# Scores of the first two batches from float32 q and k, instead of from rounded parts and rests

## The chip, the cores and the metric

The kernel runs on one core of a Trainium2 chip. The metric is the device time of one execution in microseconds (us), the median of several executions. A core has five engines that run side by side, each with its own queue taken in order: TensorE (PE in the profile, its weight loads PEld), VectorE (DVE), ScalarE (ACT), GpSimd (POOL) and SyncE (SP), which here issues all transfers (DMA).

## The reference, cut to what matters

Three layers follow each other: causal attention with a decay (4 batches, 8 heads, 576 positions, 64 numbers per head), a gated feed-forward layer of 2304 tokens, 512 wide, 1536 inside, and a layer of 8 experts (512 wide, 1024 inside) whose outputs are weighted by a balanced gate. The change touches the first line of the attention alone.

```python
def _attn_ref(q, k, v, f):
    B, H, S, D = q.shape                       # 4, 8, 576, 64
    scores = (1.0 / np.sqrt(D)) * np.matmul(q, k.transpose(0, 1, 3, 2))
    log_f = np.log(np.clip(f, 0.0001, 1.0))
    cum = np.cumsum(log_f, axis=-1)
    decay = cum[:, :, :, None] - cum[:, :, None, :]
    causal = np.triu(np.ones((S, S), dtype=bool), k=1)
    scores = np.where(causal, -1000000000.0, scores + decay)
    scores = scores - np.max(scores, axis=-1, keepdims=True)
    attn = np.exp(scores)
    attn = attn / (np.sum(attn, axis=-1, keepdims=True) + 1e-09)
    return np.matmul(attn, v)
# x = attention output, (2304, 512); then
# silu(x @ w_gate) * (x @ w_val) @ w_out; then the experts
```

## The kernel before, in words

Numbers are kept near float32 exactness by splitting a float32 matrix into a rounded part (type float32r, which TensorE takes in one pass) and a rest, the float32 value less the rounded part. Products are then sums of two or three float32r matmuls. ScalarE makes the rounded part with a copy, GpSimd the rest with a subtraction (`rest`, line 142).

The attention of one batch is `attn_unit(b)`, a list of steps: for each head `load` (lines 229 to 254), `head_a`, `front_b` and `back_b`, and after each second head a `fold` (line 347), which normalises the pair and writes the layer's input `xh`, `xl`.

- `load(h)` brings q and k of a head, transposed, 64 rows (the head's numbers) by 2 by 576, into the tile `qk` of 128 rows. It does so twice (line 231), once into rows 0 to 63 and once into rows 64 to 127. ScalarE casts the whole tile to float32r (`qkh`, line 247). GpSimd then overwrites the lower 64 rows of q with q's rest (line 249, the row `qkh<-qk,qkh` of the profile) and makes k's rest in a tile `kl` (line 250). So the contraction of 128 rows holds q rounded and q's rest, and two matmuls, one with rounded k and one with k's rest, give all four partial products.
- `scores(h, qi)` forms a strip of 128 queries against the keys up to them, in a PSUM tile `ps_s`: one chunk each for qi 0 to 3 (128, 256, 384 and 512 keys; the first runs over 256 columns), two of 288 for qi 4. A chunk is a matmul with rounded k (line 268), for the five chunks that reach the diagonal a bf16 matmul of an identity with the causal mask (line 271, 128 rows by 128 columns), and a matmul with k's rest (line 272). VectorE then adds the decay (line 274), ScalarE takes the exponent (line 278).
- `trans` transposes the strips on TensorE (line 309); for qi 4 these are transposes from the lower 64 rows. `pv` multiplies by v. In batch 0 (`first`) that product is formed directly in float32 (line 332), in the other batches from rounded parts and rests (line 340).

The program begins with `attn_unit(0)` merged with three calls of `convert`. Then `attn_unit(1)` is merged with `moe_unit(0)`, the first feed-forward of batch 0, then batch 2's attention with batch 1's feed-forward, and so on. A step of `merge` only sets the order in which the program is written; the builder then orders each engine's queue by a plan of its own before the program runs, and each engine follows that order.

`convert(i)`, called 18 times during the first two batches, loads one megabyte of feed-forward weights as 64-bit floats into `st` (line 103, two buffers), takes them apart on VectorE, ScalarE and GpSimd (lines 111 to 122), makes the rounded part and the rest (lines 124 and 142, `w<-st,w`) and writes them back for the later batches (line 126). `moe_unit` runs its matmuls through the helper `three` (line 150); the tiles `pm` and `py` are its products.

Buffers around the change: `raw` (tiles `qk` and `cb`) and `spl` (`qkh`, `kl`) have two buffers each; `ps_m` has three, `ps_s`, `ps_t` two and `ps_o` one.

Of the kernel before, what the change touches and what calls it, by code (L numbers as in the profile page):

```python
# [8 lines left out]
F32 = mybir.dt.float32  # L9
F32R = mybir.dt.float32r  # L10
# [23 lines left out]
def attention_two_ffns(ctx: ExitStack, tc: tile.TileContext, qkT, vt, f, wf, g2, w1, w2, out):  # L34
    nc = tc.nc
    B, H, D, _, S = qkT.shape
# [4 lines left out]
    P = 128  # L41
# [7 lines left out]
    def pool(name, bufs, **kw):  # L49
        return tc.tile_pool(name=name, bufs=bufs, **kw)  # L50
# [14 lines left out]
    identb = const.tile([P, P], BF16, name="identb")  # L65
# [3 lines left out]
    maskb = const.tile([P, P], BF16, name="maskb")  # L69
# [61 lines left out]
    NPE = 1  # L131
    PACE = 2
    ONV = (2, 4)

    def fetch(i):
        t = wring.tile([P, 2, 2, HP], F32R, tag="w", name="w")
        last_dma[0] = nc.sync.dma_start(out=t.bitcast(F32), in_=wsplit[i])
        return t

    def rest(out, src, hi, eng=None):  # L140

        (eng or nc.gpsimd).tensor_tensor(out=out, in0=src, in1=hi.bitcast(F32), op=ALU.subtract)  # L142
# [14 lines left out]
    raw = at_ctx.enter_context(pool("raw", 2, side="right"))  # L157
    spl = at_ctx.enter_context(pool("spl", 2, side="right"))
# [3 lines left out]
    small = at_ctx.enter_context(pool("small", 1, side="right"))  # L162
# [40 lines left out]

    def attn_unit(b):
        first = b == 0
        pairs, heads = {}, {}

        def load_pair(hp):
            if hp == 0:
                xs[b] = [(xin0, xin1)[b % 2].tile([P, KD, S], F32R, tag=t, name=t) for t in ("xh", "xl")]  # L210
                if b < 2:
                    spaces(b)
            vs = vss[hp % 2]
            vr = vs if first else vp.tile([P, 5, P], F32, tag="vr", name="vr")
            src = vt[b, :, hp * P:(hp + 1) * P]
            nc.sync.dma_start(out=vr[:, 0:4, :], in_=src[0:512].rearrange("(j p) d -> p j d", p=P))
            nc.sync.dma_start(out=vr[64:128, 4, :], in_=src[512:576])
            if not first:
                v4 = vr.rearrange("p j (h d) -> p j h d", h=2)
                nc.scalar.copy(out=vs[:, 0:4, :, 0, :], in_=v4[:, 0:4])  # L220
                for h in range(2):
                    rest(vs[:, 0:4, h, 1, :], v4[:, 0:4, h], vs[:, 0:4, h, 0, :])
                nc.scalar.copy(out=vs[64:128, 4, :, 0, :], in_=v4[64:128, 4])
                rest(vs[64:128, 4, :, 1, :], v4[64:128, 4], vs[64:128, 4, :, 0, :])
            pairs[hp] = vs, btp.tile([P, S], F32, tag="bt", name="bt", bufs=2)

        def load(h):
            qk = raw.tile([P, 2, S], F32, tag="qk", name="qk")
            src = qkT[b, h]
            for half in (slice(0, 64), slice(64, P)):  # L230
                last_qk[0] = nc.sync.dma_start(out=qk[half], in_=src)
            cb = raw.tile([P, S], F32, tag="cb", name="cb")
            r = b * H + h
            if r < NPE:

                for c0 in (0, HB):
                    ps = ps_t.tile([P, 512], F32, tag="t", name="ps_c")
                    nc.tensor.matmul(
                        out=ps[:, 0:HB], lhsT=ident[0:B * H, r:r + 1].to_broadcast([B * H, P]), rhs=ct[:, c0:c0 + HB],
                        start=True, stop=True)  # L240
                    nc.scalar.copy(out=cb[:, c0:c0 + HB], in_=ps[:, 0:HB])
            else:
                nc.sync.dma_start(out=cb, in_=cumd[r:r + 1, :].to_broadcast([P, S]))
            qkh = spl.tile([P, 2, S], F32R, tag="qkh", name="qkh")
            kl = spl.tile([P, S], F32R, tag="kl", name="kl")
            a, kh = qkh[:, 0], qkh[:, 1]
            nc.scalar.copy(out=qkh, in_=qk)

            rest(a[64:128], qk[64:128, 0], a[64:128])
            rest(kl, qk[:, 1], kh)  # L250
            mn = small.tile([P, 6], F32, tag="mn", name="mn", bufs=4)
            heads[h] = a, kh, kl, cb, mn, {}
            if h % 2 == 0:
                load_pair(h // 2)

        def scores(h, qi):
            a, kh, kl, cb, mn, nps = heads[h]
            sm, col = sms[h // 2 % 2], (h % 2 * 4 + qi if qi < 4 else 8 + h % 2)
            last = qi == 4
            qs, r0 = (448, 64) if last else (qi * P, 0)  # L260
            L = min((qi + 1) * P, S)
            pt = npp.tile([P, L], F32, tag=f"np{qi}", name="np")
            nps[qi] = pt
            chunks = ((0, 288, 288), (288, 288, 288)) if last else ((0, max(L, 256), L),)
            prev = 3.0e38
            for n, (c0, w, use) in enumerate(chunks):
                ps = (ps_m if first else ps_s).tile([P, 512], F32, tag="m" if first else "s", name="ps_s")
                nc.tensor.matmul(out=ps[:, 0:w], lhsT=a[:, qs:qs + P], rhs=kh[:, c0:c0 + w], start=True, stop=False)  # L268
                if c0 + use == L:
                    m0 = qs - c0  # L270
                    nc.tensor.matmul(out=ps[:, m0:m0 + P], lhsT=identb, rhs=maskb, start=False, stop=False)
                nc.tensor.matmul(out=ps[:, 0:w], lhsT=a[:, qs:qs + P], rhs=kl[:, c0:c0 + w], start=False, stop=True)  # L272
                m = mn[r0:P, qi + n:qi + n + 1]
                nc.vector.tensor_tensor_reduce(  # L274
                    out=pt[r0:P, c0:c0 + use], in0=ps[r0:P, 0:use], in1=cb[r0:P, c0:c0 + use], scale=-SCALE,
                    scalar=prev, op0=ALU.add, op1=ALU.min, accum_out=m)
                prev = m
            nc.scalar.activation(
                out=pt[r0:P, 0:L], in_=pt[r0:P, 0:L], func=AF.Exp, scale=-1.0, bias=prev,
                accum_out=sm[r0:P, col:col + 1])  # L280
# [20 lines left out]
        def trans(h, qi):  # L301
# [9 lines left out]
            if first:  # L311
                copy = nc.vector.tensor_copy if qi in ONV else nc.scalar.copy
                copy(out=pts[qi // 2 > 0][h % 2][:, 0:n, c:c + w], in_=pv)
# [40 lines left out]
        def head_a(h):  # L354
            scores(h, 0)
            scores(h, 1)
            trans(h, 0)
            trans(h, 1)
            pv(h, 0)

        def front_b(h):
            for t in (2, 3, 4):
                scores(h, t)
# [7 lines left out]
        for h in range(H):  # L371
            steps += [(c, lambda fn=fn, h=h: fn(h)) for c, fn in
                      ((0.3, load), (1.5, head_a), (2.0, front_b), (2.0, back_b))]
            if h % 2 == 1:
                steps.append((0.3, lambda hp=h // 2: fold(hp)))
# [97 lines left out]
    LA, LB, LC = 1.0, 1.2, 1.2  # L473
    w0 = []
    merge(attn_unit(0), [(1.0, lambda i=i: w0.append(convert(i))) for i in range(3)])
    merge(attn_unit(1), moe_unit(0, convert, group(w0)), lead=LA)
    merge(attn_unit(2), moe_unit(1), lead=LB)
    merge(attn_unit(3), moe_unit(2), lead=LC)
    at_ctx.close()
# [275 lines left out]
```

## Time and profile before

| what | value |
|---|---|
| time, median of 3 runs | 2271.68 us (2269.86 to 2273.07) |
| span of the profiled execution | 2267.1 us |
| PE busy in the span | 2224.7 us (98%), 13881 instructions |
| DVE, ACT, POOL busy | 1689.3, 852.1, 887.4 us |
| last cast of q and k for batch 1's eighth head | starts at 238.7 us |
| last write-back of converted weights | starts at 298.6 us |

How to read it: the profile is one execution on the chip. A busy time counts an instruction from its start to its end; on PE a matmul's end is modelled and matmuls overlap, so the time that one matmul takes from the engine is the distance to the start of the next, where the engine waits for nothing. The attention and the first feed-forward fill about the first 590 us, the experts the rest. "Granted clock" is the share of TensorE's 2.4 GHz; it has two levels, 2.4 and 1.2 GHz.

### The profile page before, as it was taken

Reading aid. Unit: us, or ns where it says so; the run is one execution under the profiler, and the core shown is the slowest. Engines: PE = TensorE matmul, PEld = TensorE weight load, DVE = VectorE, ACT = ScalarE, POOL = GpSimd, SP = SyncE. Lnnn points to the kernel's source line nnn. Section 1 sums busy time; section 2 is a strip of 40 time slices with the busy share of each in tenths; the row PEclk is TensorE's granted clock in tenths of the full one; section 3 lists DMA queues with packets and bytes.
Section 4 is the critical chain, followed back from the end, with each engine's and each line's share of the span. In section 5 each row is a group of like instructions: output and inputs, shape, how many; then the busy total and the mean of one; then the engine's idle time right before and its main releaser. Section 6 shows DMA issues by size and latency. Waiting matters only on the chain.

```text
span 2267.1 us, 36323 instructions
## 1 busy us (share of the span) xinstructions
PE 2224.7 (98%) x13881; PEld 2020.8 (89%) x13881; DVE 1689.3 (75%) x3385; ACT 852.1 (38%) x1952; POOL 887.4 (39%) x684
## 2 busy tenths in 40 slices
PE   7898999999999999999999999999999999999999
PEld 5698899999999888898988989889989899898897
DVE  6778854544535799887888878877788787887876
ACT  7866754454322434332322323223232232322321
POOL 6869863342423444332323323333233232332320
PEclk9999999999999999999999999999999999999999
DMA  9766664454644232111111111161111111111101
GB/s 249 204 204 217 217 228 159 164 170 146 236 161 154 89 119 94 59 56 38 47 47 38 56 38 47 49 224 56 38 47 47 38 56 38 47 47 38 56 29 52
DMA packets 105102, 232.50 MB, mean 103 GB/s; under 512 B 10672, under 2 KB 60128, under 8 KB 92896
## 3 DMA queue, kind: packets, MB, share of 16 engines
q1 hardware_dynamic: 104928, 230.18, 31.5%
q8 instruction: 109, 1.79, 0.3%
q14 instruction: 65, 0.53, 0.1%
HBM read 193.27 MB, written 36.87 MB: 102 GB/s over the span
## 4 chain that ended last, share of the span: by engine, by line
PE 85%; DMA 6%; DVE 5%; POOL 1%; ACT 1%; issue 1%; SPq 1%; POOLq 0%; DVEq 0%; ACTq 0%
PE py L150 39%; PE pa L601 30%; PE pm L150 10%; DMA st<-wf 3%; PE ps_o L340 1%; PE ps_t L309 1%; PE ps_s L272 1%; DMA xst<-xd 1%; PE ps_s L268 1%; DMA rb<-rd 1%; DVE al L616 1%; DVE np L274 0%; DMA rd<-rt 0%; DVE y L111 0%; DMA lgd<-ls 0%
## 5 line engine op out<-in xcount | busy, mean ns | idle before, releaser
L601 PE MATMUL pa<-xf,w1h 128*128 128x288 f32 x3584 | 748.8, 295 | 0.2 <-DVE u L610 0.2
L601 PEld LDWEIGHTS pa<-xf,w1h 128*128 128x128 f32 x3584 | 597.7, 188 | 37.8 <-DVE u L610 0.7
L653 DVE SCALAR_TENSOR_TENSOR acc<-py,lg,acc 128x512 f32<-128x512 f32 x531 | 395.2, 744 | 247.5 <-PE py L150 247.3
L601 PE MATMUL pa<-xf,w1l 128*128 128x288 f32 x1792 | 527.6, 295 | 0.0
L142 POOL TENSOR_TENSOR w2l<-w,w2h 128x1024 fp32r<-128x1024 f32 x64 | 154.6, 2416 | 820.5 <-ACT w2h L577 820.5
L150 PE MATMUL py<-w2h,ah 128*128 128x512 f32 x1152 | 454.2, 394 | 3.3 <-DVE acc L646 2.8
L150 PE MATMUL py<-w2l,ah 128*128 128x512 f32 x1152 | 454.1, 394 | 0.0
L150 PE MATMUL py<-w2h,al 128*128 128x512 f32 x1152 | 453.2, 393 | 0.0
L616 DVE SCALAR_TENSOR_TENSOR al<-c,ah 128x288 fp32r<-128x288 f32 x512 | 431.5, 870 | 5.4 <-ACT ah L615 4.7
L615 ACT ACTIVATE ah<-c 128x288 fp32r<-128x288 f32 x512 | 208.0, 443 | 566.4 <-PE py L150 319.5
L601 PEld LDWEIGHTS pa<-xf,w1l 128*128 128x128 f32 x1792 | 337.0, 188 | 10.6
L150 PE MATMUL pm<-xh,w 128*128 128x288 f32 x1536 | 326.3, 298 | 3.3 <-DVE xa L431 1.6
L150 PEld LDWEIGHTS py<-w2h,al 128*128 128x128 f32 x1152 | 216.3, 188 | 50.0
L150 PEld LDWEIGHTS pm<-xh,w 128*128 128x128 f32 x1536 | 252.0, 188 | 6.2 <-DVE xa L431 2.1
L150 PEld LDWEIGHTS py<-w2h,ah 128*128 128x128 f32 x1152 | 216.3, 188 | 32.6 <-DVE acc L646 3.2
L150 PEld LDWEIGHTS py<-w2l,ah 128*128 128x128 f32 x1152 | 216.3, 188 | 26.1
L150 PE MATMUL pm<-xl,w 128*128 128x288 f32 x768 | 226.2, 295 | 0.5 <-POOL xl L142 0.5
L621 ACT COPY m<-pa 128x288 f32<-128x288 f32 x128 | 50.3, 393 | 437.0 <-PE pa L601 434.8
L142 POOL TENSOR_TENSOR w1l<-w,w1h 128x256 fp32r<-128x256 f32 x192 | 162.3, 873 | 125.1 <-ACT w1h L573 125.1
L150 PE MATMUL py<-ah,w 128*128 128x288 f32 x768 | 174.6, 299 | 4.8 <-DVE th L413 2.5
L142 POOL TENSOR_TENSOR al<-th,ah 128x288 fp32r<-128x288 f32 x96 | 83.6, 871 | 203.0 <-ACT ah L415 200.7
L142 POOL TENSOR_TENSOR w1l<-sm,w1h 128x1024 fp32r<-128x1024 f32 x64 | 153.7, 2401 | 2.5 <-ACT w1h L573 2.5
(145 smaller groups left out, 3109.4 us busy)
## 6 DMA issues: line engine op xcount, KB each, us to landing
w<-w SPq DMA_DIRECT2D x128, 512.0 KB, 3.5
w<-wsplit SPq DMA_DIRECT2D x54, 1024.0 KB, 5.5
qk<-qkT SPq DMA_DIRECT2D x64, 288.0 KB, 6.2
st<-wf SPq DMA_DIRECT2D x18, 1024.0 KB, 8.7
wsplit<-w SPq DMA_DIRECT2D x18, 1024.0 KB, 4.7
cb<-cumd SPq DMA_DIRECT2D x31, 288.0 KB, 4.0
xo<-h SPq DMA_DIRECT2D x28, 288.0 KB, 2.2
xf<-xo SPq DMA_DIRECT2D x14, 576.0 KB, 10.1
```

What stands on the lines that cost most here:

```text
L142: (eng or nc.gpsimd).tensor_tensor(out=out, in0=src, in1=hi.bitcast(F32), op=ALU.subtract)
L150: nc.tensor.matmul(out=ps, lhsT=a, rhs=b, start=(i == 0), stop=(i == n - 1))
L268: nc.tensor.matmul(out=ps[:, 0:w], lhsT=a[:, qs:qs + P], rhs=kh[:, c0:c0 + w], start=True, stop=False)
L272: nc.tensor.matmul(out=ps[:, 0:w], lhsT=a[:, qs:qs + P], rhs=kl[:, c0:c0 + w], start=False, stop=True)
L309: nc.tensor.transpose(pv[:, j, :], pt[r0:P, k0:k0 + P], ident[r0:P, r0:P])
L340: nc.tensor.matmul(out=po[:, c0:w], lhsT=vs[:, j, e].rearrange("p a d -> p (a d)"), rhs=pts[rng][part][:, j, c0:w], start=(i == 0), stop=( ...
L601: nc.tensor.matmul(out=ps, lhsT=w[:, MW[m - 1], k], rhs=x[:, m - 1, hl, k], start=(n == 0), stop=(n == len(ops) - 1))
L615: nc.scalar.activation(out=ah[:, f, tk], in_=src, func=AF.Relu)
L616: nc.vector.scalar_tensor_tensor(out=al[:, f, tk], in0=src, scalar=0.0, in1=ah[:, f, tk].bitcast(F32), op0=ALU.max, op1=ALU.subtract)
L621: nc.scalar.copy(out=m1, in_=p1)
L653: nc.vector.scalar_tensor_tensor(out=a, in0=py, scalar=lg[:, t, e:e + 1], in1=a, op0=ALU.mult, op1=ALU.add)
```

## The change

For batches 0 and 1 (`EXACT = 2`) the scores are formed from q and k as they come, in float32. There is one `qk` tile for a pair of heads: the even head's q and k go into rows 0 to 63, the odd head's into rows 64 to 127, with one transfer for each head in place of two. The cast and the two rests are left out. A chunk is one float32 matmul with a contraction of 64 rows, over just the keys it uses (128 columns for qi 0, not 256), and the mask's matmul, which keeps its 128 rows and bf16. Batches 2 and 3 go as before.

```diff
+    EXACT = 2
 ...
     def attn_unit(b):
         first = b == 0
-        pairs, heads = {}, {}
+        exact = b < EXACT
+        pairs, heads, qks = {}, {}, [None]
 ...
         def load(h):
-            qk = raw.tile([P, 2, S], F32, tag="qk", name="qk")
+            if h % 2 == 0 or not exact:
+                qk = qks[0] = raw.tile([P, 2, S], F32, tag="qk", name="qk")
+            qk = qks[0]
             src = qkT[b, h]
-            for half in (slice(0, 64), slice(64, P)):
+            rows = slice(64 * (h % 2), 64 * (h % 2) + 64)
+            for half in (rows,) if exact else (slice(0, 64), slice(64, P)):
                 last_qk[0] = nc.sync.dma_start(out=qk[half], in_=src)
 ...
-            qkh = spl.tile([P, 2, S], F32R, tag="qkh", name="qkh")
-            kl = spl.tile([P, S], F32R, tag="kl", name="kl")
-            a, kh = qkh[:, 0], qkh[:, 1]
-            nc.scalar.copy(out=qkh, in_=qk)
-
-            rest(a[64:128], qk[64:128, 0], a[64:128])
-            rest(kl, qk[:, 1], kh)
             mn = small.tile([P, 6], F32, tag="mn", name="mn", bufs=4)
-            heads[h] = a, kh, kl, cb, mn, {}
+            if exact:
+                heads[h] = qk[rows, 0], qk[rows, 1], None, cb, mn, {}
+            else:
+                qkh = spl.tile([P, 2, S], F32R, tag="qkh", name="qkh")
+                kl = spl.tile([P, S], F32R, tag="kl", name="kl")
+                a, kh = qkh[:, 0], qkh[:, 1]
+                nc.scalar.copy(out=qkh, in_=qk)
+
+                rest(a[64:128], qk[64:128, 0], a[64:128])
+                rest(kl, qk[:, 1], kh)
+                heads[h] = a, kh, kl, cb, mn, {}
 ...
-                nc.tensor.matmul(out=ps[:, 0:w], lhsT=a[:, qs:qs + P], rhs=kh[:, c0:c0 + w], start=True, stop=False)
-                if c0 + use == L:
+                masked = c0 + use == L
+                if exact:
+                    w = use
+                nc.tensor.matmul(
+                    out=ps[:, 0:w], lhsT=a[:, qs:qs + P], rhs=kh[:, c0:c0 + w], start=True, stop=exact and not masked)
+                if masked:
                     m0 = qs - c0
-                    nc.tensor.matmul(out=ps[:, m0:m0 + P], lhsT=identb, rhs=maskb, start=False, stop=False)
-                nc.tensor.matmul(out=ps[:, 0:w], lhsT=a[:, qs:qs + P], rhs=kl[:, c0:c0 + w], start=False, stop=True)
+                    nc.tensor.matmul(out=ps[:, m0:m0 + P], lhsT=identb, rhs=maskb, start=False, stop=exact)
+                if not exact:
+                    nc.tensor.matmul(
+                        out=ps[:, 0:w], lhsT=a[:, qs:qs + P], rhs=kl[:, c0:c0 + w], start=False, stop=True)
```

## Rows read from the trace of the kernel before

**Rows 1.** The page's first line.

```profile
span 2267.1 us, 36323 instructions
```

**Rows 2.** Windows: stretch, length, engines' busy us (instructions), granted clock, DMA share, GB/s.

```profile
10.00:112.00 102.00, 88.14 (x484) 67.44 (x484) 77.11 (x196) 80.62 (x196) 78.80 (x58) 0.94 0.82 227
112.00:315.00 203.00, 192.78 (x1384) 178.21 (x1383) 160.54 (x360) 138.58 (x326) 163.50 (x130) 0.98 0.67 218
315.00:590.00 275.00, 273.49 (x2056) 263.88 (x2055) 134.99 (x367) 131.53 (x325) 97.46 (x95) 1.00 0.50 168
```

**Rows 3.** PE by line, 10 to 112 us: busy, mean ns, idle before, its releasers.

```profile
L268 PE MATMUL ps_s<-qkh 128*128 128x256 f32 (+2 forms) x68 | 28.6, 430 | 10.5 <-DVE mn L274 8.6 <-POOL qkh L142 1.3 <-DVE pt L313 0.4
L272 PE MATMUL ps_s<-kl,qkh 128*128 128x256 f32 (+2 forms) x66 | 26.2, 418 | 1.8 <-POOL kl L142 1.8
```

**Rows 4.** Lines by form, 0 to 260 us: the cast and the two rests.

```profile
L142 POOL TENSOR_TENSOR kl<-qk,qkh 128x576 fp32r<-128x576 f32 x20 | 34.4, 1721 | 1.6
L142 POOL TENSOR_TENSOR qkh<-qk,qkh 64x576 fp32r<-64x576 f32 x21 | 31.7, 1509 | 19.4 <-ACT qkh L247 16.9 <-issue 1.3
L247 ACT CAST qkh<-qk 128x1152 fp32r<-128x1152 f32 x21 | 24.2, 1155 | 3.5 <-DMA qk<-qkT 1.9 <-PE ps_s L272 1.5
```

**Rows 5.** The page's DMA issues: count, KB each, us to landing.

```profile
qk<-qkT SPq DMA_DIRECT2D x64, 288.0 KB, 6.2
```

**Rows 6.** The chain that ended last, in time: start us, us, what.

```profile
92.67 1.42 POOL qkh L142
94.18 2.27 POOL kl L142
```

**Rows 7.** PE timeline, 55.5 to 58.3 us: start us, us, line and form.

```profile
55.59 0.44 PE L268 MATMUL ps_s<-qkh 128*128 128x384 f32 x1
...
56.17 0.39 PE L268 MATMUL ps_s<-qkh 128*128 128x512 f32 x1
...
56.76 0.29 PE L268 MATMUL ps_s<-qkh 128*128 128x288 f32 x1
...
57.02 0.27 PE L288 MATMUL ps_r<-ident,rc 128*10 128x128 f32 x1
...
57.70 0.38 PE L268 MATMUL ps_s<-qkh 128*128 128x288 f32 x1
...
58.18 0.27 PE L309 MATMUL ps_t<-ident,np 128*128 128x128 f32 x1
```

**Rows 8.** PE timeline, 26.9 to 32 us: chunks of 256 columns.

```profile
27.07 0.36 PE L268 MATMUL ps_s<-qkh 128*128 128x256 f32 x1
...
27.52 0.28 PE L268 MATMUL ps_s<-qkh 128*128 128x256 f32 x1
...
27.88 0.34 PE L268 MATMUL ps_s<-qkh 128*128 128x384 f32 x1
```

**Rows 9.** PE timeline, narrow stretches from 23.6 us: float32 matmuls of line 332.

```profile
23.61 0.60 PE L332 MATMUL ps_o<-pt,vs 128*128 128x320 f32 x2
...
23.88 0.74 PE L332 MATMUL ps_o<-pt,vs 128*128 128x192 f32 x3
...
24.30 0.43 PE L332 MATMUL ps_o<-pt,vs 64*128 64x64 f32 x2
...
24.66 0.81 PE L332 MATMUL ps_o<-pt,vs 128*128 128x320 f32 x2
...
25.03 0.70 PE L332 MATMUL ps_o<-pt,vs 128*128 128x320 f32 x2
```

**Rows 10.** PE timeline, 432 to 437 us: transposes from 64 rows in feed-forward matmuls.

```profile
432.67 0.29 PE L150 MATMUL pm<-xh,w 128*128 128x288 f32 x1
432.89 0.46 PE L309 MATMUL ps_t<-ident,np 64*128 64x64 f32 x4
433.28 0.40 PE L150 MATMUL pm<-xh,w 128*128 128x288 f32 x1
433.52 0.29 PE L150 MATMUL pm<-xl,w 128*128 128x288 f32 x1
```

## The prediction

> **What bounds the kernel now.** I read the windows first, because the change touches only the heads of batches 0 and 1. All their scores lie before 315 us. From 10 to 112 us PE is busy 88.1 of 102 us, DVE 77.1, ACT 80.6, POOL 78.8; from 112 to 315 us PE is busy 192.8 of 203 us, POOL 163.5 [rows 2]. So PE is the fullest engine in both stretches, with 13.9 and 10.2 us of idle time, 24.1 us in all. After 315 us it is busy 273.5 of 275 us [rows 2], and whatever is late at 315 us stays late to the end. The clock is granted at 0.94 and 0.98 of full speed in the two stretches [rows 2]. With two levels, 2.4 and 1.2 GHz, a mean of 0.94 means that 12% of 102 us went at the lower one, which loses half of that, 6.1 us; by the same working the second stretch loses 4.1 us. What PE could win back without having less to do is thus at most 24.1 + 10.2 = 34 us.
>
> Then I looked for what PE's idle time waits on. In the first stretch the score matmuls have 10.5 us of idle ahead of line 268, 8.6 of it until VectorE has read a chunk and frees its PSUM buffer, and 1.8 us ahead of line 272. Only 1.3 + 1.8 = 3.1 us of it ends with GpSimd's rests [rows 3]. The chain that ended last does pass through the rests of a head, 1.42 and 2.27 us [rows 6]: they stand in POOL's queue between other work that the feed-forward waits for.
>
> **What is taken away.** For each of 16 heads, one cast of 1.16 us on ACT and two rests of 1.51 and 1.72 us on POOL [rows 4]: 18.5 us of ACT and 51.7 us of POOL. Also one transfer of 288 KB of the two that each head has now [rows 5], and with it an issue on SP's queue. None of these engines is the fullest, so this gives time back only through PE's idle time. Its direct part is the 3.1 us above; the indirect part is VectorE and the weight conversion being less late.
>
> **The scores on PE before.** I take distances between starts where nothing waits. The masked chunk of 384 takes 0.58 us (55.59 to 56.17), that of 512 0.59, the unmasked 288 0.26, the masked 288 0.48 [rows 7], and the two that run over 256 columns 0.45 and 0.36 [rows 8]. A head's scores thus take 2.72 us of PE. Rounded matmuls of 288 columns alone, at 0.13 us each (two in 0.26 us [rows 7]), would make 1.79 us of the 2 x 1984 columns, so the masks and the changes between matmuls already cost 0.93 us.
>
> **The scores on PE after.** Batch 0's product with v is in float32 today, and its rows price the new form. One float32 matmul stands there as two records (the block of 64 rows is one matmul of the program and has x2), and a record of 320 columns takes 0.27 us (23.61 to 23.88) [rows 9]. That is 0.54 us for 320 columns, twice per column what the two rounded matmuls together take now. A head uses 128 + 256 + 384 + 512 + 2 x 288 = 1856 columns: 3.13 us.
>
> The second part is the change of shape. The scores will contract 64 rows, the mask between them keeps 128. The trace has such changes. Around the 64-row block of line 332, two records of 192 columns take 0.42 us where 0.32 is due, the two of 64 columns 0.36 where 0.11 is due, and the next record 0.37 in place of 0.27 [rows 9]: 0.45 us for going to 64 rows and back. Around the transposes from 64 rows, the matmul before takes 0.22 and the one after 0.24 us where 0.13 is due [rows 10]: 0.20 us, without what is lost in between. In the float32 block some of the loss in between comes from records too short to cover the next weight load, which the longer score records are not. I take 0.35 us for there and back, and 0.06 us for the mask's own 128 columns. Each of the five masked chunks of a head pays both, 2.05 us. The unmasked one pays only where other work stands behind it, as it does at 57.02 us [rows 7]; I take half, 0.17 us. Sum: 3.13 + 2.05 + 0.17 = 5.35 us, 2.63 more than now, and 42 us for 16 heads.
>
> Bounds: if the changes of shape cost no more than today's masks and changes (0.93 us), a head takes 4.06 us, 1.34 more, 21 us in all. If all six chunks pay 0.45 us, it is 3.13 + 2.7 + 0.3 = 6.13 us, 3.41 more, 55 us in all. I keep near the middle, since rows 9 and 10 are the very same transitions with longer or shorter neighbours. The heads differ in rows (0 to 63, 64 to 127); the rows show only the lower half, and I take the same for both.
>
> **What of it is hidden.** PE is the fullest engine, so the 42 us lie on the path, save for what fills idle time. Of the 24.1 us idle I let 16 go: the 3.1 us of rests wholly, of the rest somewhat over half, because other engines get ahead while PE is busier and POOL is lighter. Of the 10 us lost to the clock I take 4 back, as fewer gaps lie ahead of a fall. That leaves 42 - 16 - 4 = +22 us. The span would be 2267.1 [rows 1] + 22 = 2289 us; the median of the runs lies 4.6 us over that span, so 2271.7 + 22 = 2294 us.
>
> A wait is added too: the pair's tile is held until both heads' scores have read it, where the cast and the rests let it go early. SP takes its queue in order, so the weights of `convert`, the decay rows and the pair's reciprocals stand behind a q and k transfer that waits for its buffer. Two buffers now hold four heads, so I price it at nothing, up to the idle time that I otherwise let go, 16 us.
>
> **The rivals.**
> - *The relief wins* (faster). Rests on the chain [rows 6] and POOL at 163.5 of 203 us [rows 2] speak for it: the weight conversion could set the pace. It needs the 34 us of idle and lost clock to come back and the added work to be near its lower bound: 2271.7 + 21 - 34 = 2259 us. It decides below 2.1 us added for a head (34 / 16). Against it stand rows 9 and 10 and the fact that even then PE would have no idle at all. Chance 0.07.
> - *The two halves run side by side* (no change). If an even and an odd head's matmuls were at work at once, a head's 3.13 us would come to 1.57, the added 2.63 to 1.06, 17 us in all, and with 20 given back the time is 2271.7 - 3 = 2269 us. No row shows two halves at once; the heads are written one after the other and a mask of 128 rows parts any two masked chunks. Chance 0.05. On this the Trainium skill ("TensorEngine Tiling (Array Packing)", Key Properties) says that different tiles of the array can load and multiply in parallel, but also that changing the tiling mode drains TensorE. By the first the scores would get cheaper, as in this rival; the second speaks against the change, and rows 9 and 10 agree with it, with 0.20 to 0.45 us there and back.
> - *Nothing is hidden and the upper price holds* (slower still), through SP's queue as above: 2271.7 + 55 = 2327 us. Chance 0.10.
>
> **How the numbers follow.** My forecast, 2294 us, has chance 0.78. Its own range comes from its terms: 21 added with 16 given back is +5, 55 with 12 given back is +43. The 8-in-10 range reaches a little below that for the second rival, 2272 to 2316, and leaves out the first and the third. A measurement of this kernel can tell about 0.2% (4.5 us) from no change. Faster by more: 0.07. Within it, the second rival and the lowest end of my own case: 0.10. Slower: 0.83.
>
> **What would show it.** Line 268 with two records for a chunk and no line 272 in batches 0 and 1; starts of the two records of a 512-column chunk 0.43 us apart; about 0.4 us more than the passes for a masked chunk. POOL some 50 us lighter before 330 us, PE with less than 10 us idle from 10 us on, and the last weight write-back some 20 us after 298.6 us; from there on no difference. I am wrong if a head's scores take under 4.8 us, or if the first feed-forward ends no later than now.

## The result, and the profile after

The changed kernel takes 2282.9 us (median of 5 runs, 2280.7 to 2286.1) against 2271.7 us: 1.0064 times the kernel before, with a 95% interval of 1.0049 to 1.0079. By the recorded ratio the change is 14.5 us slower (11 to 18). The two medians named here lie 11.2 us apart, the profiled spans 14.0 us, and the medians of a later repeat (e11 below) 13.8 us. The forecast was 22 us.

The page's totals of the changed kernel: first its span, then each engine's busy us, share and instructions.

```profile
span 2281.1 us, 36210 instructions
PE 2256.3 (99%) x13881; PEld 2016.2 (88%) x13881; DVE 1682.2 (74%) x3385; ACT 837.7 (37%) x1936; POOL 831.0 (36%) x652
```

POOL is 56 us lighter than the 887.4 us of before, ACT 14 us. PE is busy 31.6 us longer than the 2224.7 us of before, and its idle time (span less busy) falls from 42.4 to 24.8 us. The work went to the fullest engine, as forecast, and part of it filled idle time. The windows of the changed kernel answer to [rows 2]; I cut the first stretch at 41 us for a reason that comes below.

```profile
10.00:41.00 31.00, 28.75 (x72) 15.07 (x73) 20.57 (x43) 16.53 (x41) 12.98 (x11) 1.00 0.83 255
41.00:112.00 71.00, 71.00 (x343) 42.22 (x342) 40.39 (x120) 43.46 (x116) 22.60 (x19) 1.00 0.46 138
112.00:315.00 203.00, 197.95 (x1329) 170.26 (x1328) 152.53 (x342) 126.22 (x298) 137.50 (x115) 0.99 0.62 208
315.00:590.00 275.00, 275.00 (x2085) 265.54 (x2084) 139.67 (x394) 141.84 (x355) 104.38 (x101) 1.00 0.51 168
```

PE has no idle time at all from 41 to 112 us, and the granted clock, 0.94 and 0.98 before, is 1.00 and 0.99. That share counts from the first clock record on, and there is none in the first 40 us here; what went on there has to be read from durations. A mask matmul is always of one shape. In PE's timeline of the kernel before (start us, us, line and form) it takes 0.33 us until 20.03 us and 0.23 us from 20.43 us on:

```profile
20.03 0.33 PE L271 MATMUL ps_s<-maskb,identb 128*128 128x128 bf16 x1
...
20.43 0.23 PE L271 MATMUL ps_s<-maskb,identb 128*128 128x128 bf16 x1
```

In that of the changed kernel the short form comes at 41 us only:

```profile
34.34 0.29 PE L283 MATMUL ps_s<-maskb,identb 128*128 128x128 bf16 x1
...
41.38 0.23 PE L283 MATMUL ps_s<-maskb,identb 128*128 128x128 bf16 x1
```

The chain that ended last shows how large this is. These are the ten records of the second part of one head's product with v, for a head early and a head later in the changed kernel (start us, us, what):

```profile
34.63 4.86 PE ps_o L346 x10
47.06 2.58 PE ps_o L346 x10
```

The same ten matmuls take 4.86 and then 2.58 us: TensorE ran at the lower of its two levels, 1.2 GHz. The trace's clock records put the rise to 2.4 GHz at 40.8 us, and at 20.3 us before. It was not idle meanwhile: from 10 to 41 us it is busy 28.75 of 31 us, in 72 instructions.

Where the 14 us come out is not where they go in. The write of each batch's first feed-forward output, in SP's timeline of the changed kernel:

```profile
312.83 0.54 SPq L450 DMA_DIRECT2D xd<-xa  x1
469.39 0.33 SPq L450 DMA_DIRECT2D xd<-xa  x1
629.83 0.32 SPq L450 DMA_DIRECT2D xd<-xa  x1
754.19 0.33 SPq L450 DMA_DIRECT2D xd<-xa  x1
```

And of the kernel before:

```profile
311.91 0.38 SPq L436 DMA_DIRECT2D xd<-xa  x1
472.45 0.38 SPq L436 DMA_DIRECT2D xd<-xa  x1
617.16 0.32 SPq L436 DMA_DIRECT2D xd<-xa  x1
739.59 0.33 SPq L436 DMA_DIRECT2D xd<-xa  x1
```

Batch 0 comes out 0.9 us later than before and batch 1 3 us earlier. The attention of the next batch, which runs beside each feed-forward, falls behind instead: the last mask matmul of the eighth head of batch 1 starts at 251.3 us (201.7 before), of batch 2 at 434.3 us (364.4 before). Batches 2 and 3 come out 13 and 15 us late. These times also set right a row ahead of the prediction: the cast at 238.7 us is the twentieth, so it belongs to batch 2, and batch 1's eighth head has its cast at 180.5 us. Before the change, the part of the second stretch from 202 to 315 us thus held none of the scores that change.

### The profile page after: what moved, and what is told of

It reads as the page before. It is cut to its first block, busy times and chain, and to the rows that moved or that the text cites. A ratio compares the mean times of both kernels' runs of the same rounds, so it can differ in the third digit from the quotient of the medians.

```text
span 2281.1 us, 36210 instructions
## 1 busy us (share of the span) xinstructions
PE 2256.3 (99%) x13881; PEld 2016.2 (88%) x13881; DVE 1682.2 (74%) x3385; ACT 837.7 (37%) x1936; POOL 831.0 (36%) x652
## 4 chain that ended last, share of the span: by engine, by line
PE 92%; DVE 3%; DMA 3%; POOL 1%; issue 1%; ACT 0%; SPq 0%; DVEq 0%; POOLq 0%; ACTq 0%
PE py L151 40%; PE pa L615 29%; PE pm L151 12%; PE ps_s L279 3%; PE ps_t L323 2%; PE ps_o L354 2%; DMA st<-wf 1%; PE ps_o L346 1%; PE ps_s L285 1%; PE ps_s L283 1%; DVE al L630 1%; DMA xst<-xd 1%; DVE xt L519 0%; DMA rd<-rt 0%; DVE c L624 0%
```

## The experiments

In all of them a head's tile can hold q and k in one of two ways: "64 rows" is the change; "128 rows" keeps the float32 matmul but contracts 128 rows, with zeros in q's lower half, so that no matmul of the scores changes shape. The 128 rows bring more with them: a tile for each head, a second transfer and a memset on POOL. Ratios are to the kernel before, run on the same chip; 0.001 is 2.3 us.

| kernel | batch 0 | batch 1 | ratio (95% interval) | mask short from |
|---|---|---|---|---|
| before | rounded parts | rounded parts | 1 | 20.4 us |
| the change | 64 rows | 64 rows | 1.0064 (1.0049 to 1.0079) | 41.4 us |
| e11, the change again | 64 rows | 64 rows | 1.0063 (1.0048 to 1.0078) | 41.5 us |
| e1 | 128 rows | 128 rows | 0.9991 (0.9980 to 1.0002) | 18.9 us |
| e2 | 64 rows | as before | 1.0009 (0.9999 to 1.0019) | 41.5 us |
| e5 | as before | 64 rows | 1.0019 (1.0006 to 1.0032) | 16.7 us |
| e6 | 128 rows | as before | 0.9959 (0.9946 to 0.9973) | 19.7 us |
| e7 | 128 rows | 64 rows | 1.0021 (1.0002 to 1.0040) | 17.2 us |
| e8 | 64 rows | 128 rows | 1.0030 (1.0018 to 1.0042) | 40.8 us |
| e9 | 128 for two heads, then 64 | 64 rows | 0.9996 (0.9986 to 1.0006) | 19.4 us |
| e12 | 128 for two heads, then 64 | as before | 0.9959 (0.9946 to 0.9973) | 17.8 us |
| e3, no rests | rounded parts | rounded parts | 0.9984 (0.9973 to 0.9994) | 13.2 us |
| e4, the change with rests | 64 rows | 64 rows | 1.0082 (1.0067 to 1.0097) | 29.8 us |
| e10, e6 with rests | 128 rows | as before | 0.9973 (0.9961 to 0.9985) | 18.7 us |

The last column is the first mask matmul with the short duration after the start, as in the rows above. In e7 and e12 the clock records also have 3.4 us at full speed from 10 us on, in which no mask matmul lies.

### Shape or passes: e1

```diff
-            if h % 2 == 0 or not exact:
-                qk = qks[0] = raw.tile([P, 2, S], F32, tag="qk", name="qk")
...
+            qk = raw.tile([P, 2, S], F32, tag="qk", name="qk")
...
+            if exact:
+                nc.gpsimd.memset(qk[64:128, 0], 0.0)
+                last_qk[0] = nc.sync.dma_start(out=qk[0:64], in_=src)
+                nc.sync.dma_start(out=qk[64:128, 1], in_=src[:, 1])
...
-                heads[h] = qk[rows, 0], qk[rows, 1], None, cb, mn, {}
+                heads[h] = qk[:, 0], qk[:, 1], None, cb, mn, {}
```

> The float32 scores as in the changed kernel, but with a contraction of 128 rows: q's lower 64 rows are zeros, set by GpSimd for each head, k lies in both halves, and each head has its own tile. So the passes stay and the going to 64 rows and back is gone; a memset of 64x576 on POOL and one more transfer of 144 KB come for each head. If the change of shape costs PE what the changed kernel's rows suggest (about 0.2 us inside a chunk and 0.1 around it, 1.5 to 2 us for a head, 24 to 32 us for 16 heads) and two thirds of it lie on the path, the time falls from 2283 to 2262 to 2270 us. If the passes alone make the loss, it stays at 2283 within 4. If the 64-row matmuls are what holds the clock at 1.2 GHz for the first 41 us, the clock rises near 20 us here, as in the kernel before; if it stays at 41 us, the float32 scores or the order of the start do it.

Measured 0.9991, 2268.7 us: 16 us under the change, though the passes are the same. So the float32 passes alone make no loss. Besides the tiles, transfers and memsets, two things differ: the shape, and the clock, which is up at 19 us here. This run can't tell them apart.

### Which batch: e2 and e5

```diff
-    EXACT = 2
+    EXACT = 1
```

> The change for batch 0 alone. If PE is the bound in both batches alike, half of the loss of 11 us stays: 2277 us. If batch 0 has the idle time that absorbs the scores (13.9 us idle from 10 to 112 us before), batch 0's share is nearly free and the time is 2270 to 2274 us. If the loss sits in batch 0, where the clock stayed low for 41 us, it is 2280 to 2284 us.

Measured 1.0009, 2272.2 us, with the clock up at 41 us.

e5 does the opposite: `WIDTH = (0, 64, 0, 0)` gives each batch its rows, and `exact` is `width > 0`.

> The change for batch 1 alone, batch 0 as before. The change for batch 0 alone measured 2272, 1.6 us over the kernel before; both together 1.0064 times the kernel before, 14.5 us. If the two add up, batch 1 costs 13 us: 2283 to 2284. If the loss needs both (the late rise of the clock in batch 0 together with the heavier scores in batch 1), batch 1 alone costs 4 to 8 us: 2275 to 2279 us. The clock rises near 20 us, as in the kernel before, since the heads at the start have 128 rows.

Measured 1.0019, 2275.0 us: 4.3 us. The two alone come to 6.4 us, less than half of the 14.5 us of both. The two don't add up to the whole. That would fit shares that depend on how full the other batch leaves PE, but no run shows the reason.

### What the relief is worth: e3, e4 and e10

e3 leaves the two rests out of the kernel before and uses the rounded parts in their place; the scores lack those parts.

```diff
-            kl = spl.tile([P, S], F32R, tag="kl", name="kl")
             a, kh = qkh[:, 0], qkh[:, 1]
             nc.scalar.copy(out=qkh, in_=qk)
-
-            rest(a[64:128], qk[64:128, 0], a[64:128])
-            rest(kl, qk[:, 1], kh)
+            if b < 2:
+                kl = kh
+            else:
+                kl = spl.tile([P, S], F32R, tag="kl", name="kl")
+                rest(a[64:128], qk[64:128, 0], a[64:128])
+                rest(kl, qk[:, 1], kh)
```

> The kernel before, in which batches 0 and 1 leave out the two rests of q and k: q's lower half is rounded q again and the second matmul uses rounded k, so the scores are sums of the wrong parts. PE's work and the cast stay as they are and POOL loses about 3.2 us for each of 16 heads. If the relief of POOL is what gave PE's idle time back, as the forecast has it, this gains 10 to 18 us against 2272: 2254 to 2262 us. If POOL's work was hidden, and the idle time fell only because PE had more to do, the time stays within 4 us of 2272.

Measured 0.9984: 3.7 us gained (1.4 to 6), less than the 10 to 18 us of the relief's case. In the profiled run PE's idle time, 41.0 us, is that of before (42.4). e4 puts the cast and the rests back into the changed kernel, unread.

```diff
                 heads[h] = qk[rows, 0], qk[rows, 1], None, cb, mn, {}
+                qkh = spl.tile([P, 2, S], F32R, tag="qkh", name="qkh")
+                kl = spl.tile([P, S], F32R, tag="kl", name="kl")
+                nc.scalar.copy(out=qkh[rows], in_=qk[rows])
+                rest(qkh[rows, 0], qk[rows, 0], qkh[rows, 0])
+                rest(kl[rows], qk[rows, 1], qkh[rows, 1])
```

> The changed kernel, with the cast and the two rests of each head of batches 0 and 1 still made, for nobody: ACT and POOL carry what they carried before, PE has the float32 scores. If the relief gave 10 to 18 us back, the time rises from 2283 to 2293 to 2300 us. If the relief is worth nothing, it stays within 4 us of 2283.

Measured 1.0082 against 1.0064: about 4 us, with intervals that overlap. Its totals:

```profile
span 2288.0 us, 36279 instructions
PE 2257.8 (99%) x13881; PEld 2017.8 (88%) x13881; DVE 1685.3 (74%) x3385; ACT 853.9 (37%) x1952; POOL 882.8 (39%) x684
```

POOL is back at 882.8 us, yet PE's idle time is 30.2 us, not the 42.4 of before: 12 of the 17.6 us of idle that vanished vanish without any relief. PE having more to do is the cause that is left. e10 does the same to e6, the kernel with 128 rows in batch 0.

> Float32 scores for batch 0 alone with 128 rows, which ran in 2260.6 us, 9 us under the kernel before, with the cast and both rests of batch 0's heads still made, for nobody. If the gain is the relief of ACT and POOL in batch 0, all of it goes: 2269 to 2273 us. If it comes from PE (float32 scores without the second set of loads, fewer waits for the rests), 2261 to 2265 us.

Measured 0.9973 against 0.9959: 3 of its 9 us go. So e3 has 3.7 us for 53 us of POOL alone, e4 4 us for 52 us of POOL and 16 us of ACT, and e10 3 us for 22 us of POOL and 7 us of ACT. In e4 and e10 the intervals overlap those of the kernels they are held against, so neither of these two alone tells the relief apart from nothing; 3 to 4 us is the best estimate of the three.

### Shape in one batch: e6, e7 and e8

The edit of e1, for batch 0 alone (e6, e7) or batch 1 alone (e8).

> Float32 scores for batch 0 alone, with a contraction of 128 rows (q's lower half zeros, own tile for each head); batches 1 to 3 as before. With 64 rows that was 2272. If the shape changes of batch 0 lie on the path, half of the 16 us that 128 rows gave for both batches is gained: 2262 to 2266 us, which would beat both kernels. If batch 0 hides them in idle time, it stays at 2270 to 2273 us. The clock should rise near 18 us.

> The changed kernel with 128 rows in batch 0 and 64 rows in batch 1. If shape changes alone make the loss and weigh alike in both batches, half of 16 us is gained against the change: 2276 to 2278 us. If a good part of the loss is the clock that stays at 1.2 GHz until 41 us, which batch 0's first heads decide, nearly all of that part is gained here: 2269 to 2273 us, with the clock up near 18 us.

> The changed kernel with 64 rows in batch 0 and 128 rows in batch 1, the mirror of the run before. If shape changes weigh alike in both batches: 2276 to 2278 us. If the clock at the start is a good part of the loss, little is gained: 2279 to 2283 us, with the clock still low until about 41 us.

Measured 0.9959, 1.0021 and 1.0030. 64 rows in place of 128 cost 11.4 us in batch 0 when batch 1 is as before (e2 over e6), and 7.7 us in batch 1 when batch 0 has 64 rows (the change over e8), with the clock late in both kernels. I had expected about 8 us in each if the shapes alone make the loss. By their medians, 2275.0 and 2277.0 us, e7 and e8 lie nearer to that case (2276 to 2278 us) than to the case of the clock (2269 to 2273 and 2279 to 2283 us). e7's runs lie far apart, 2266 to 2285 us, and its profiled run, one of the longest, has the clock granted at 0.97 even from 315 to 640 us, where all others have 0.99 or 1.00; I rest nothing on it. But it speaks, if anything, against the sum drawn below, by which it should lie near e9's 0.9996.

### The clock or the shapes: e9 and e12

```diff
         def load(h):
+            width = 128 if first and h < 2 else WIDTH[b]
```

> The changed kernel, with a contraction of 128 rows for the first two heads of batch 0 alone. So far all four kernels with 64 rows in batch 0 have the clock up late (29 to 41 us), the five with 128 rows there at 10 to 20 us. Two heads' shape changes are worth 2 to 3 us. If the late clock is what the 64-row scores of batch 0 cost, moving it to 20 us gives 20 us at double speed back, 8 to 12 us: 2272 to 2276 against 2283. If the clock comes up early and the time falls by 2 to 3 us only, the low clock of the start is hidden or given back later; if the clock stays low, it is not the first heads that decide it.

Measured 0.9996, 2267.7 us. Fourteen of the sixteen heads are as in the change, and 15 us are gone, more than the 8 to 12 us that I had put on the clock. The same product with v as above, in this kernel's chain:

```profile
24.04 2.56 PE ps_o L352 x10
33.47 2.56 PE ps_o L352 x10
```

> Float32 scores for batch 0 alone: 128 rows for the first two heads, 64 rows for the other six; batches 1 to 3 as before. With 64 rows for all eight it was 2272 (1.0009 times the kernel before) with the clock low until 40.5 us, with 128 rows for all eight 2260.6 (0.9959) with the clock up at 18.7 us. If the late clock is the whole difference of those two, this comes to 2258 to 2263 us with the clock up near 18 us. If the shape changes of heads 2 to 7 are the difference, it stays at 2268 to 2272 us though the clock is up early.

Measured 0.9959, e6's ratio: with the clock up at 18 us, the shape changes of heads 2 to 7 cost no more than the intervals of the two ratios leave open (3 us each), and the 11.4 us between e2 and e6 go with the first two heads. The clock is up 23 us earlier than in e2; 23 us at half speed are 11.5 us of lost work, which is about that sum. In e9 against the change it is 15 us. There, 23 us between the rises (17.7 and 40.8 us) make 11.5 us, and 1.7 us are a fall of 3.4 us from 279.8 us on, which e9's clock records don't have. The rest, some 2 us, can be the two heads' own changes of shape, which I had put at 2 to 3 us; no run shows it.

So with the clock up early the ratios split the change thus: batch 0 in float32 gains 9.3 us (e12), batch 1 gives 8.4 us back (e9 over e12), and the first two heads, with the late clock, add 15 us. Each of these carries about 4 us of uncertainty.

**A version that beats both** is e12 or e6, float32 scores in batch 0 alone with the first heads at 128 rows: 2259.7 and 2260.6 us, 0.9959 of the kernel before (a gain of 0.4%, clear of the interval) and 23 us under the change. e12's totals:

```profile
span 2256.4 us, 36265 instructions
PE 2227.1 (99%) x13881; PEld 2012.2 (89%) x13881; DVE 1679.8 (74%) x3385; ACT 845.9 (37%) x1944; POOL 859.5 (38%) x670
```

PE is busy 2.4 us longer than before and idle 29.3 us in place of 42.4: batch 0's float32 scores fit into idle time and into a clock that rises earlier and falls less.

> The changed kernel itself, beside the two others on one chip: 2280 to 2286 us, 1.005 to 1.008 times the kernel before.

It measured 1.0063, 2283.4 us, which confirms the first result beside e9 and e10 on one chip.

## Why the prediction was right or wrong, point by point

**Bound right, direction by luck in good part.** PE was the fullest engine, and work moved to it came out as time. But in e9, with the same scores in fourteen of sixteen heads and an early clock, the change measures 0.9996 (0.9986 to 1.0006): no change. That it came out slower rests on a late clock that I had not foreseen.

**The price of a chunk: right to a tenth.** PE's timeline in the changed kernel, a masked chunk of 384 and one of 512 (start us, us, line and form; two records of a chunk are merged in a row):

```profile
50.69 0.91 PE L279 MATMUL ps_s<-qk 64*128 64x384 f32 x2
51.53 0.23 PE L283 MATMUL ps_s<-maskb,identb 128*128 128x128 bf16 x1
51.69 1.12 PE L279 MATMUL ps_s<-qk 64*128 64x512 f32 x2
52.75 0.23 PE L283 MATMUL ps_s<-maskb,identb 128*128 128x128 bf16 x1
52.91 0.75 PE L279 MATMUL ps_s<-qk 64*128 64x288 f32 x2
```

They take 1.00 us (50.69 to 51.69) and 1.22 us (51.69 to 52.91). My formula, 0.54 us for 320 columns and 0.41 for shape and mask, gives 1.06 and 1.27. The reading of [rows 9] and [rows 10] held in size. It did not hold in place: I had said that the two records of a 512-column chunk would start 0.43 us apart, and they start 0.53 us apart (51.69 and 52.23 us), so a part of the price of the shape lies between the records of a chunk, where I had put none.

**The sum for the heads: too large.** I had 42 us. PE's busy time rose by 31.6 us, of which the clock makes about 2 (below): 29.5 us, 1.8 us for a head in place of 2.63. The score matmuls by themselves show where the difference lies. Summed by distances between starts, with waits left out, a head of batch 1 takes 4.5 to 4.9 us in the changed kernel, 4.74 on the mean, where I had 5.35; before, it takes 2.7 to 3.4 us, 3.04 on the mean, where I had summed 2.72 from stretches where nothing waits [rows 7, 8]. So 0.6 us of my excess is on the new side and 0.3 on the old. What a change of shape costs the work ahead of a chunk is not in that count.

**The idle time: right in size, and mostly by one of the two causes.** I let 16 us of the 24.1 go; from 10 to 315 us 16.8 went, in the whole span 17.6. I named two causes, a busier PE and a lighter POOL. e4 shows that 12 us of it go without the second. The relief is worth 3 to 4 us. This is also why the first rival, in which the relief wins, had little ground in POOL's busy time of 163.5 us [rows 2].

**The clock: the step that failed.** I took 4 us back, as fewer falls of the clock. The later falls did go nearly all, 10.2 us of loss down to 2. But the rise at the start came 20.5 us later, which loses 10.3 us. Net 2 us lost, where I had a gain of 4. I had read the clock only as a loss later on, from a share that says nothing of the start, though the longer durations of the first 20 us stood in the trace. The runs go further: e9 and e12 show that the two heads that bring the late rise are worth as much as the whole loss. It is not the only place where the loss could be taken back: e8 gains 7.7 us on the change by the rows of batch 1, with the clock still late.

The sum by the measured terms is 29.5 - 17.6 + 2 = 14 us, the difference of the spans. The forecast's 42 - 16 - 4 came as near to it as it did because two errors ran against each other: the heads 12.5 us too dear, the clock 6 us too kind.

**What would show it.** POOL is lighter by the 50 us I named, and PE's idle time from 10 to 315 us is 7.3 us, under 10. But I had said I'd be wrong if a head's scores took under 4.8 us, and by the count above they do, narrowly; and if the first feed-forward ended no later than now. It ended at nearly the same time (312.8 after 311.9 us), and the last weight write-back, which I had put 20 us later, hardly moved (299.3 after 298.6 us). Two moves hide in that. In e9, with the clock up early, batch 0 comes out 27 us sooner than in the kernel before:

```profile
284.95 0.33 SPq L456 DMA_DIRECT2D xd<-xa  x1
```

So with the clock up early the float32 scores let the first feed-forward finish sooner, and the first two heads with the late clock put that back. The kernel is slower all the same: it is batches 2 and 3 that come out late. With PE full until 590 us, a loss can be handed on through several batches, and the place to look for it was the third batch, not the first.

**The rivals.** "The relief wins" named 2259 us, and half of the change does land there: batch 0 alone, with an early clock, at 2259.7 us. Its condition was idle time and clock coming back, and that is what e12 shows, with the relief as the smaller part. That the two numbers meet is chance: the rival's was for both batches at the lowest price. "The two halves run side by side" did not occur between score matmuls. It did occur between a score matmul and transposes from 64 rows, in PE's timeline of the changed kernel:

```profile
44.46 0.34 PE L323 MATMUL ps_t<-ident,np 64*128 64x64 f32 x2
44.59 0.51 PE L279 MATMUL ps_s<-qk 64*128 64x288 f32 x1
44.64 0.35 PE L323 MATMUL ps_t<-ident,np 64*128 64x64 f32 x3
44.93 0.40 PE L279 MATMUL ps_s<-qk 64*128 64x288 f32 x1
```

Three transposes start between the two records of a 288-column chunk, and these are 0.35 us apart, as they are without transposes between them (52.91 and 53.26 us). The added wait on the pair's tile does not show among PE's waits from 10 to 315 us.

**What stays open.** Why the heads with 64 rows hold the clock down at the start, while the same heads do not bring it down later: from 41 to 112 us the changed kernel runs them at full clock. In e4, which has them too, the clock records have the rise at 29.1 us already, and a fall from 42.8 to 49.6 us, after PE had waited:

```profile
41.08 0.75 PE L284 MATMUL ps_s<-qk 64*128 64x288 f32 x2 [1.70 <-DVE mn L293]
```

Nor is it shown that the rows as such decide it. In every kernel with the clock up early the first heads also have a tile each and two transfers, and no run has the one without the other. Whether other full-height work on TensorE ahead of the first scores would raise the clock was not tried.

## What to carry to other kernels

Work that moves from a relieved engine to the fullest one must be priced in that engine's own time, from rows of the same operation elsewhere in the trace, and the relief counted only as far as a run shows it: here 70 us taken off two engines were worth about 4 us. Put exact but costly forms where the fullest engine has idle time (here batch 0), not where it is already fed by other streams (here batch 1). And read the start of a kernel by the durations of one fixed operation: here TensorE ran at half speed for the first 20 us before and the first 41 us after, and the granted clock of the windows did not say so.

## What the runs showed of the hardware

The five kernels whose batch 0 begins with 64-row float32 scores (the change, e11, e2, e8, e4) reach the short mask at 29.8 to 41.5 us; the nine that begin with 128 rows, rounded or float32, at 13.2 to 20.4 us. PE was no busier before the rise in the one than in the other. These are the windows from 10 us to the rise of the kernel before (20.3 us), of the kernel before and of the changed one:

```profile
10.00:20.30 10.30, 7.85 (x30) 5.94 (x29) 6.61 (x16) 5.52 (x14) 3.79 (x3) 1.00 1.04 235
10.00:20.30 10.30, 8.05 (x17) 3.58 (x18) 7.00 (x16) 5.13 (x12) 2.71 (x2) 1.00 0.88 242
```

The changed kernel was then busy without a pause to its own rise at 40.8 us. What the speed is worth shows in e9, whose clock is up at 17.7 us:

```profile
10.00:41.00 31.00, 29.66 (x129) 17.70 (x129) 21.64 (x61) 22.84 (x59) 10.24 (x9) 1.00 0.77 234
```

In the same 31 us the changed kernel got through 72 matmul instructions, e9 through 129. Two heads of full height at the very start, with what comes with them, decided 15 us of 2283.
